# Sums of activations for the down-products: one set of hidden channels at a time, or two sets in one VectorE operation

## The chip, the cores and the metric

The kernel runs on one core of one Trainium2 chip. The metric is the device time in microseconds of one execution; lower is better. A run is called fast here when its time is within 1.5% of the fastest of the same kernel. TensorE is called PE in the profile, its weight loads PEld, VectorE DVE, ScalarE ACT, GpSimd POOL.

## The reference, cut to what matters

A linear-attention layer on 8 batches of 1024 tokens gives `x` (1024 x 512 for each batch). A mixer follows, and its second half is the part that matters here:

```python
h  = np.maximum(xt @ w_tok1, 0.0) @ w_tok2      # over tokens
u  = x + h.transpose(0, 2, 1)
h2 = np.maximum(u @ w_ch1, 0.0) @ w_ch2         # 512 -> 1536 -> 512 channels
return (u + h2).astype(np.float32)
```

## The kernel before

The two channel products are each made with seven products of half-size blocks in place of eight (a Strassen-Winograd scheme). The tokens are cut into 16 blocks `j`. In each, the 1536 hidden channels are done in three sets `m`: `up_set(j, m)` makes seven up-products into three PSUM banks (`x`, `y`, `z`), rectifies them into `G`, and makes the four sums of activations that the down-products need. Then `down_block(j)` makes seven down-products over all three sets. The title of the change speaks of heads; what it touches are these sets.

```python
SINGLE = 2
TOTALS = ((), (0, 1), (2,))
...
    def up_set(j, m):
        ...
        def total(n, a, b, add):
            f = nc.vector.tensor_add if add else nc.vector.tensor_sub
            c = slice(2 * both[0], 2 * both[-1] + 2)
            dve(
                512 * len(both), lambda: f(out=G[:, n, c], in0=G[:, a, c], in1=G[:, b, c]), ps=False,
                reads=[("G", j % 2, i, mm) for i in (a, b) for mm in both],
                writes=[("G", j % 2, n, mm) for mm in both],
            )
        ...   # seven up-products, rectified by ACT (relu) or DVE (add_relu) into G
        both = TOTALS[m] if SINGLE <= j < NSB - 1 else (m,)     # NSB = 16
        if both:
            total(3, 5, 2, True)
            total(5, 0, 5, False)
            total(4, 3, 0, False)
            total(6, 1, 4, False)
    ...
    def down_block(j):
        ...
                jobs.append(pe(
                    C2, 256, lambda t=t: mm(n, t),          # C2 = 6 matmuls
                    reads=w + [("G", j % 2, G_OF[n], m) for m in range(SETS)],   # all three sets
                    ...
        # order of the products: 1, 7, 6, 2, 5, 3, 4
```

Nothing is issued in the order in which it is written. `pe(...)`, `dve(...)` and `act(...)` add jobs with an assumed duration and dependences to a list, and a planner orders all of them on all engines before the program is built. So a change in one kind of job can change the order everywhere.

The softmax here doesn't subtract the row's maximum and nothing guards it: scores larger than these inputs give would overflow.

## Time and profile before

| | before |
|---|---|
| time, median of 3 runs | 423.13 us (423.12 to 423.6) |
| span in the profile | 421.2 us |
| TensorE busy | 412.1 us, 98% |
| VectorE busy | 348.0 us, 83% |
| sums of activations on VectorE | 52 of 1024 elements, 88 of 512 |

The lines are shown in the prediction. How to read them: in a group's line come line, engine, operation, output and inputs, shapes and count, then busy time in all, mean nanoseconds of one, and the idle time just ahead of them. In the trace of this kernel the printed duration of a VectorE operation reaches past the start of the next by 0.083 us (median of the 587 that are followed without a gap); for the wide sums the printed mean is 0.681 us and the median distance to the next start 0.602 us. What an operation takes from the engine is therefore read from the distance of two starts. An eviction is an operation of VectorE or ScalarE that reads a finished product out of its PSUM bank; the program lets the next product into that bank only after it.

### The profile page before, as it was taken

The page shows a single profiled execution, that of the slowest core. Times are in us where ns is not written, and L with a number is a line of the kernel's source. Part 1 is how long each engine was busy: PE and PEld are TensorE (multiplying, and loading weights), DVE is VectorE, ACT ScalarE, POOL GpSimd, SP SyncE. Part 2 cuts the span into 40 slices and gives each one's busy share as a digit, 9 for nine tenths or more (in the row PEclk, how much of TensorE's full clock was granted, in tenths as well). Part 3 has the DMA queues.
Part 4 walks back from the last instruction along what each step waited for, and adds up shares of the span by engine and source line. Part 5 has one row for each costly group of instructions (what it writes and reads, how often), then busy time and mean ns, then how long its engine had stood idle before and what let it go on. Part 6 is the DMA issues. An engine that isn't in the chain of part 4 may idle for free.

```text
span 421.2 us, 9421 instructions
## 1 busy us (share of the span) xinstructions
PE 412.1 (98%) x3838; PEld 347.7 (83%) x3838; DVE 348.0 (83%) x747; ACT 231.8 (55%) x444; POOL 66.2 (16%) x104
## 2 busy tenths in 40 slices
PE   7999999999999999999999999999999999999996
PEld 3587877688788888888798888888898899988885
DVE  2359969679679798988889899898988798997685
ACT  1858884475636546564645556655646645354530
POOL 8453220022003030022103020212100000010110
PEclk9999999999999999999999999999999999999999
DMA  9999999996975989398974989999760501250223
GB/s 166 207 201 206 207 206 164 225 177 140 216 145 103 195 133 235 64 186 141 207 163 94 191 139 224 163 200 179 153 146 0 152 27 76 50 151 2 102 100 103
DMA packets 96668, 62.48 MB, mean 148 GB/s; under 512 B 62064, under 2 KB 92272, under 8 KB 96624
## 3 DMA queue, kind: packets, MB, share of 16 engines
q0 software_dynamic: 34944, 45.09, 54.5%
q1 hardware_dynamic: 61056, 16.00, 21.6%
q10 hardware_dynamic: 624, 0.79, 0.7%
q8 instruction: 30, 0.49, 0.5%
q14 instruction: 14, 0.11, 0.1%
HBM read 59.24 MB, written 16.78 MB: 180 GB/s over the span
## 4 chain that ended last, share of the span: by engine, by line
PE 91%; DVE 4%; ACT 2%; DMA 1%; issue 0%; DVEq 0%
PE psum L1253 34%; PE psum L1144 33%; PE psum L848 4%; PE psum L484 4%; PE psum L597 3%; PE psum L964 3%; PE psum L656 2%; DMA o<-in_F_dram 1%; PE psum L620 1%; DVE u L1071 1%; PE psum L736 1%; PE psum L687 1%; PE psum L581 1%; PE psum L405 1%; PE psum L711 1%; PE psum L1032 1%
## 5 line engine op out<-in xcount | busy, mean ns | idle before, releaser
L1253 PEld LDWEIGHTS <-G 128*128 128x128 bf16 x1344 | 130.6, 98 | 19.7 <-issue 1.5
L1253 PE MATMUL psum<-wc_sb,G 128*128 128x256 bf16 x768 | 102.5, 273 | 0.5 <-ACT psum L1309 0.2
L1166 ACT ACTIVATE G<-psum 128x512 bf16<-128x512 f32 x96 | 57.3, 600 | 56.0 <-PE psum L1144 55.4
L1144 PEld LDWEIGHTS <-wc_sb 128*128 128x128 bf16 x768 | 73.8, 98 | 10.9 <-issue 0.6
L1253 PE MATMUL psum<-wT,G 128*128 128x256 bf16 x576 | 77.7, 273 | 0.1
L1180 DVE TENSOR_TENSOR G<-G 128x512 bf16<-128x512 bf16 (+1 forms) x140 | 69.5, 516 | 1.0
L1144 PEld LDWEIGHTS <-wT 128*128 128x128 bf16 x576 | 55.7, 98 | 9.0 <-issue 1.2
L1144 PE MATMUL psum<-uT,wc_sb 128*128 128x256 bf16 x384 | 57.7, 273 | 0.2 <-ACT psum L1187 0.2
L1144 PE MATMUL psum<-S,wc_sb 128*128 128x256 bf16 x384 | 57.6, 273 | 0.1
L1144 PE MATMUL psum<-S,wT 128*128 128x256 bf16 x384 | 55.6, 273 | 0.4 <-DVE S L781 0.4
L1287 POOL DMA_DIRECT2D out_dram<-o x30 | 16.4, 548 | 240.2 <-DVE o L1293 125.6
L1125 DVE CUSTOM_DVE_ANT_0 G<-psum,ub 128x512 bf16<-128x512 f32 x48 | 32.9, 685 | 15.3 <-PE psum L1144 15.1
L1172 ACT COPY ua<-psum 128x512 f32<-128x512 f32 x48 | 28.2, 588 | 30.1 <-PE psum L1144 29.7
L606 ACT ACTIVATE a<-psum 128x512 bf16<-128x512 f32 x64 | 36.4, 602 | 12.4 <-PE psum L597 11.8
L1293 DVE TENSOR_TENSOR o<-psum,u 128x512 f32<-128x512 f32 x55 | 37.5, 683 | 6.4 <-PE psum L1253 6.3
L1187 ACT COPY psum<-psum 128x512 f32<-128x512 f32 x48 | 27.8, 580 | 18.9 <-DVE G L1125 9.9
L1125 DVE CUSTOM_DVE_ANT_0 G<-psum,ua 128x512 bf16<-128x512 f32 x48 | 32.7, 682 | 5.0 <-ACT ua L1172 4.6
L1172 ACT COPY ub<-psum 128x512 f32<-128x512 f32 x48 | 28.2, 588 | 7.0 <-PE psum L1144 6.3
L1144 PE MATMUL psum<-uT,wT 128*128 128x256 bf16 x192 | 28.8, 273 | 0.1
L673 DVE TENSOR_TENSOR x_sb<-psum,rdn 128x512 bf16<-128x512 f32 x40 | 27.4, 686 | 0.6
L597 PE MATMUL psum<-qT,kT 128*128 128x512 bf16 x64 | 21.5, 380 | 0.6 <-ACT kT L549 0.6
L346 POOL DMA_DIRECT2D v_sb<-in_v_dram x18 | 13.5, 749 | 50.7 <-DMA uT<-u 48.0
(108 smaller groups left out, 547.2 us busy)
## 6 DMA issues: line engine op xcount, KB each, us to landing
out_dram<-o POOLq DMA_DIRECT2D x30, 512.0 KB, 4.2
k_sb<-in_k_dram POOLq DMA_DIRECT2D x14, 512.0 KB, 8.5
v_sb<-in_v_dram POOLq DMA_DIRECT2D x14, 512.0 KB, 10.3
q_sb<-in_q_dram POOLq DMA_DIRECT2D x14, 512.0 KB, 9.9
wc_sb<-in_moe_w_ch_dram POOLq DMA_DIRECT2D x6, 256.0 KB, 12.3
wc_sb<-in_moe_w_ch_dram POOLq DMA_DIRECT2D x4, 384.0 KB, 12.3
k_sb<-in_k_dram POOLq DMA_DIRECT2D x4, 256.0 KB, 6.8
v_sb<-in_v_dram POOLq DMA_DIRECT2D x4, 256.0 KB, 7.3
```

What stands on the lines that cost most here:

```text
L484: nc.tensor.matmul(t[0:KP, 0:hn], ET_sb[:, si, :], k_sb[:, hs, si, :], start=a, stop=z)
L597: lambda: nc.tensor.matmul(bank(bk), kT[:, h].rearrange("p c k -> p (c k)"), qT[:, h].rearrange("p j s -> p (j s)"), start=True, stop=True,),
L606: lambda: nc.scalar.activation(out=a_t[h // 2 % 2][:, h % 2], in_=bank(bk), func=ACT.Exp, scale=scale),
L673: lambda: nc.vector.tensor_tensor(out=x_sb[:, :, h * D : (h + 1) * D].rearrange("p (n c) d -> p n c d", n=2), in0=view()[:, :, :, 0:D], in ...
L1125: nc.vector._custom_dve(TENSOR_ADD_SAT, out=out, in0=in0, in1=in1, s0=FMAX, s1=0.0)
L1144: nc.tensor.matmul(t[:, c, :], w1_of(n, dd, 2 * m + c), a_of(j, n, dd), start=(n in (1, 7) and c == 0 and dd == 0), stop=(c == 1 and dd == 1),
L1166: lambda: nc.scalar.activation(out=G[:, n, cs], in_=view(src), func=ACT.Relu),
L1172: 512, lambda: nc.scalar.copy(out=dst, in_=view("y")), writes=[(name, s % 2)],
L1180: 512 * len(both), lambda: f(out=G[:, n, c], in0=G[:, a, c], in1=G[:, b, c]), ps=False,
L1187: 512, lambda: nc.scalar.copy(out=view("y"), in_=view("x")), takes=[bk["y"]],
L1253: nc.tensor.matmul(to, G[:, G_OF[n], cc, t * P : (t + 1) * P], w2_of(n, cc), start=(n in opens and (t == 0 or alone) and cc == 0), stop=(c ...
L1293: 512, lambda: nc.vector.tensor_add(out=dst, in0=view(src), in1=u_of(sh, dh)),
```

## The change

Its intent: never make the sums for two sets in one operation, so that those of set 0 can run earlier and each piece is shorter. The whole diff is one number, which makes the condition on `j` false for every block:

```diff
-SINGLE = 2
+SINGLE = 99
 TOTALS = ((), (0, 1), (2,))
```

## The prediction

The trace of the kernel before shows the pace: behind a matmul of 256 columns the median distance to the next start is 0.109 us (0.109 to 0.110 from the 10th to the 90th percentile).

> **What bounds the kernel now.** I read the page's first part first, then the busy time by stage, then the groups of TensorE by shape, then stretches of the timeline, and last the list of waits.
>
> ```profile
> PE 412.1 (98%) x3838; PEld 347.7 (83%) x3838; DVE 348.0 (83%) x747; ACT 231.8 (55%) x444; POOL 66.2 (16%) x104
> ...
> PE 91%; DVE 4%; ACT 2%; DMA 1%; issue 0%; DVEq 0%
> ```
>
> TensorE (PE) is busy for 98% of the span and carries 91% of the chain that ended last. VectorE (DVE), the engine that the change loads, is second with 83%. The stages, with the columns of busy microseconds by engine:
>
> ```profile
> core 0: us, PE busy (x) PEld busy (x) DVE busy (x) ACT busy (x) POOL busy (x), PEclk, DMA share, GB/s
> 0.00:60.00 60.00, 55.83 (x598) 41.92 (x599) 39.25 (x109) 41.35 (x92) 26.67 (x43) 1.00 1.20 198
> 60.00:400.00 340.00, 339.19 (x3090) 290.95 (x3088) 293.99 (x610) 186.45 (x346) 38.43 (x59) 1.00 0.73 143
> 400.00:421.20 21.20, 17.08 (x155) 14.82 (x153) 14.77 (x29) 4.00 (x7) 1.07 (x2) 1.00 0.28 100
> ```
>
> From 60 to 400 us TensorE is idle for 340 - 339.19 = 0.8 us in all, with a granted clock of 1.00. VectorE is busy there for 293.99 / 340 = 86%. A busy TensorE need not be at its peak, so I checked the pace in the timeline of TensorE:
>
> ```profile
> 183.17 0.60 PE L1144 MATMUL psum<-S,wT 128*128 128x256 bf16 x4
> 183.61 0.60 PE L1144 MATMUL psum<-uT,wc_sb 128*128 128x256 bf16 x4
> 184.04 0.60 PE L1144 MATMUL psum<-S,wc_sb 128*128 128x256 bf16 x4
> 184.48 0.82 PE L1253 MATMUL psum<-wc_sb,G 128*128 128x256 bf16 x6
> ...
> 186.00 0.82 PE L1253 MATMUL psum<-wT,G 128*128 128x256 bf16 x6
> ```
>
> Four matmuls of 256 columns start 0.44 us apart (183.17 to 183.61), so 0.109 us each, and the next group starts with no gap. The up-products (L1144) and the down-products (L1253) have 1344 of them each; 2688 x 0.109 = 293 us, 70% of the span. The middle of this kernel is a dense stream of matmuls, and only what opens a gap in it, or lengthens the start or the tail, can move the time.
>
> [...] The timeline of VectorE:
>
> ```profile
> 175.59 0.68 DVE L1180 TENSOR_TENSOR G<-G 128x1024 bf16<-128x1024 bf16 x1
> 176.19 0.68 DVE L994 TENSOR_TENSOR u<-psum,x_sb 128x512 bf16<-128x512 f32 x1
> ...
> 184.45 0.42 DVE L1180 TENSOR_TENSOR G<-G 128x512 bf16<-128x512 bf16 x1
> 184.78 0.42 DVE L781 TENSOR_TENSOR S<-uT,S 128x512 bf16<-128x512 bf16 x1
> ```
>
> A wide sum takes 176.19 - 175.59 = 0.60 us of the engine, a narrow one 184.78 - 184.45 = 0.33 us. Taken over all places in the trace where such a sum has a direct successor, the medians are 602 and 336 ns. The printed 0.68 and 0.42 have some 0.08 us of tail under the next operation. [...]
>
> **The change part by part.** There are 16 blocks, each with three sets of hidden channels (the "heads" of the change's title are these sets: a third of the columns of the up-weights), and each block needs four sums of activations for the seven-product scheme. Blocks 0, 1 and 15 make them set by set already: 3 x 3 x 4 = 36 narrow operations. Blocks 2 to 14 make them for sets 0 and 1 together after set 1 and for set 2 alone: 13 x 4 = 52 wide and 52 narrow. The groups by shape have exactly this:
>
> ```profile
> L1180 DVE TENSOR_TENSOR G<-G 128x512 bf16<-128x512 bf16 x88 | 35.3, 418 | 0.7
> L1180 DVE TENSOR_TENSOR G<-G 128x1024 bf16<-128x1024 bf16 x52 | 35.2, 681 | 0.3
> ```
>
> Removed: 52 wide sums, 52 x 0.602 = 31.3 us of VectorE. Added: 104 narrow ones, 104 x 0.336 = 34.9 us. Net +3.6 us over the run, 0.28 us per block of about 23.4 us (the wide sums of blocks 2 and 14 lie 281 us apart, over 12 blocks), or 1.2% of VectorE. By printed durations the group would grow by 104 x 0.418 - 52 x 0.681 = 8.1 us, but 0.08 us of each of the 52 extra ones lies under a neighbour. VectorE then goes from 294 to about 297.6 us busy in the 340 us, 87.5%. Idle time of the engine is 46 us there, so the 3.6 us fit without becoming the bound.
>
> Moved: the sums of set 0 may now run once its own rectified products exist, about 8 us (a third of a block) before those of set 1. That makes no product ready sooner, because each down-product sums over all three sets and so waits for set 2. In the block shown, the wide sums stood at 175.59 to 179.26, and the first product that reads one (L1253 with wT) starts at 186.00, so they had 6 us or more to spare; set 2's sum at 184.45 had about one. The tight one is not changed in shape. A narrow sum also holds the in-order VectorE for 0.34 us where a wide one held it for 0.60, so an eviction that becomes ready behind it is later by 0.27 us less.
>
> Moved too: the kernel orders all its work by a planner before it is built, so other durations and dependences give another order on every engine from block 2 on. The TensorE work is the same, 3838 matmuls. On the path that sets the end, the sum is 0 us from the work itself, plus what the new order opens or closes in gaps.
>
> **The rivals.** First, *VectorE becomes the bound in its fullest stretches*. For it: it is at 18.8 to 19.0 of 20 us in three of the 20-us stretches (160 to 180 and 220 to 260), where 0.24 us more per 20 us is a sixth to a fifth of what is left. Its lateness would appear as PSUM banks freed late, so TensorE gaps. If the whole 3.6 us came through, the time would be 426.7. Against: the list of waits has TensorE waiting for hardly any VectorE work after the start:
>
> ```profile
> PE psum L1144 <- DVE S L781: 0.4, 1, 0.4
> PE psum L1253 <- ACT psum L1309: 0.2, 1, 0.2
> PE psum L1144 <- ACT psum L1187: 0.2, 1, 0.2
> PE psum L1253 <- DVE o L1293: 0.2, 1, 0.2
> ```
>
> and one wait of 0.4 us of a weight load for a sum (L1180). So a delay of some tenths is mostly taken up by the other PSUM banks; I expect 0 to 1 us of it.
>
> Second, *finer pieces help*: sums of set 0 fill small idle times earlier, and evictions wait less. What speaks against a large gain is the ceiling: 0.8 us of idle TensorE in the middle, so at best about 422.3.
>
> Third, *the new order meets an accident*: a transposed load or an eviction in another turn, and a single TensorE gap of one to several microseconds, or a longer tail than now. The page cannot exclude it. The old setting was presumably chosen because it was no slower, which leans me the same way. That would make 424 to 427. The tail itself belongs to block 15, which is set by set in both kernels.
>
> **Range and chances.** The work on TensorE gives 423.1 unchanged. I add 0.3 us for VectorE's load and 0.3 us for the mean harm of a new order, which is my guess between "nothing" and the third rival. So I predict 423.7 us, 8 times in 10 between 422.3 (all middle gaps closed) and 426.2 (most of the added 3.6 us on the path). A gain of 2% would be 8.5 us, ten times the idle there is to win in the middle: chance 0.01. A loss of 2% needs more than twice the added VectorE time on the path: 0.03. Within 2%: 0.96.
>
> **What would show it.** In the changed kernel the sums should be one group of 192 narrow operations of about 418 ns with no wide ones; VectorE's busy time near 351.6 us (+3.6) in 799 instructions; TensorE with the same 3838 matmuls and 412 to 413 us busy; and the idle of TensorE from 60 to 400 us still under 2 us. If that idle grew to 3 us or more with waits for VectorE evictions (L1125, L1293, L994) or for ACT copies behind them, the first rival is right. If one wait of over a microsecond stood for the difference, or one for a DMA, it is the third. If the first 60 or the last 20 us changed in length by more than 0.5 us, my view that only the middle is touched is wrong.

Three statements in it rest on readings that it does not print; all are from the trace of the kernel before. That a busy TensorE need not be at its peak: from 60 to 400 us the starts of matmuls come late by 3.9 us in all against the trace's own pace, where the stage shows 0.8 us of idle time. That VectorE works in order: all 747 operations start in the order of the built program (in the changed kernel all 799). That other PSUM banks take up a delay: from 60 to 400 us there are 322 cases in which VectorE was the last to read a bank, and the next matmul into that bank started 0.59 us (median) after VectorE's printed end, in 275 cases at least 0.3 us after it. That this takes up most of a delay was an estimate; the experiments give the price.

## The result

The changed kernel took 422.80 us (median of 4 runs, 422.75 to 423.41), the kernel before 423.22 us (4 runs). The ratio of the fast runs is 0.9992, with a 95% interval of 0.9975 to 1.0009: no difference shown. A ratio here is formed within the rounds in which both kernels ran, so it is not quite the ratio of the medians quoted. A second comparison, in the experiments, gave 1.0005.

The page and the stages (0 to 60, 60 to 400 and the end) of the changed kernel:

```profile
PE 411.3 (98%) x3820; PEld 347.7 (83%) x3838; DVE 352.3 (84%) x799; ACT 231.2 (55%) x444; POOL 66.2 (16%) x104
```

```profile
0.00:60.00 60.00, 55.67 (x592) 41.66 (x597) 39.19 (x109) 41.17 (x91) 26.67 (x43) 1.00 1.20 199
60.00:400.00 340.00, 338.32 (x3076) 291.00 (x3088) 298.89 (x664) 186.01 (x347) 38.49 (x59) 1.00 0.73 142
```

The sums, by shape, in its groups:

```profile
L1180 DVE TENSOR_TENSOR G<-G 128x512 bf16<-128x512 bf16 x192 | 77.1, 421 | 2.6
```

Where they stand, in its timeline of VectorE; this is the block whose wide sums stood at 175.59 to 179.26 before:

```profile
166.27 0.41 DVE L1180 TENSOR_TENSOR G<-G 128x512 bf16<-128x512 bf16 x1
166.60 0.68 DVE L1000 TENSOR_TENSOR u<-psum,a 128x512 bf16<-128x512 f32 x1
167.20 0.42 DVE L1180 TENSOR_TENSOR G<-G 128x512 bf16<-128x512 bf16 x1
```

VectorE has 799 - 747 = 52 operations more and is busy 352.3 - 348.0 = 4.3 us more. The first sums of this block run 9.3 us earlier (166.27 against 175.59). TensorE, which carries the chain to the end, is as full as it was: 338.32 of 340 us in the middle against 339.19. The 0.9 us between them are partly a gap in the record: the trace after has 3820 matmul records and 3838 weight loads, so 18 matmuls that ran are missing. The change did to VectorE all that it was meant to do, and the time did not move.

### The profile page after: what moved, and what is told of

The parts are those of the page before. It is cut to its first block, busy times and chain, and to the rows that moved or that the text cites. A ratio compares the mean times of both kernels' runs of the same rounds, so it can differ in the third digit from the quotient of the medians.

```text
span 421.4 us, 9457 instructions
## 1 busy us (share of the span) xinstructions
PE 411.3 (98%) x3820; PEld 347.7 (83%) x3838; DVE 352.3 (84%) x799; ACT 231.2 (55%) x444; POOL 66.2 (16%) x104
## 4 chain that ended last, share of the span: by engine, by line
PE 89%; DMA 4%; DVE 3%; issue 1%; POOL 1%; ACT 1%; POOLq 0%; DVEq 0%
PE psum L1253 35%; PE psum L1144 34%; PE psum L848 5%; PE psum L964 4%; PE psum L484 3%; DMA q_sb<-in_q_dram 3%; PE psum L597 2%; PE psum L656 2%; DMA v_sb<-in_v_dram 2%; DVE u L1071 1%; PE psum L687 1%; PE psum L620 1%; PE psum L736 1%; PE psum L711 1%; PE psum L581 1%
## 5 line engine op out<-in xcount | busy, mean ns | idle before, releaser
L1253 PEld LDWEIGHTS <-G 128*128 128x128 bf16 x1344 | 130.2, 98 | 19.5 <-issue 1.6
L1253 PE MATMUL psum<-wc_sb,G 128*128 128x256 bf16 x768 | 103.0, 273 | 0.6 <-DVE wait L1293 0.4
L1144 PEld LDWEIGHTS <-wc_sb 128*128 128x128 bf16 x768 | 74.2, 98 | 10.3 <-issue 0.3
L1180 DVE TENSOR_TENSOR G<-G 128x512 bf16<-128x512 bf16 x192 | 77.1, 421 | 2.6
L1253 PE MATMUL psum<-wT,G 128*128 128x256 bf16 x576 | 77.5, 273 | 0.5
L1144 PEld LDWEIGHTS <-wT 128*128 128x128 bf16 x576 | 55.7, 98 | 10.0 <-issue 1.4
L1144 PE MATMUL psum<-uT,wc_sb 128*128 128x256 bf16 x384 | 57.7, 273 | 0.1
L1144 PE MATMUL psum<-S,wc_sb 128*128 128x256 bf16 x384 | 57.6, 273 | 0.2
L1144 PE MATMUL psum<-S,wT 128*128 128x256 bf16 x384 | 56.1, 273 | 0.5 <-DVE S L781 0.4
L1125 DVE CUSTOM_DVE_ANT_0 G<-psum,ub 128x512 bf16<-128x512 f32 x48 | 33.0, 687 | 15.7 <-PE psum L1144 15.4
L1125 DVE CUSTOM_DVE_ANT_0 G<-psum,ua 128x512 bf16<-128x512 f32 x48 | 33.1, 689 | 11.0 <-ACT ua L1172 10.7
L1293 DVE TENSOR_TENSOR o<-psum,u 128x512 f32<-128x512 f32 x55 | 37.6, 686 | 1.9 <-PE psum L1253 1.5
L1144 PE MATMUL psum<-uT,wT 128*128 128x256 bf16 x192 | 28.8, 273 | 0.2
L346 POOL DMA_DIRECT2D k_sb<-in_k_dram x18 | 13.6, 758 | 62.0 <-PE psum L964 33.0
```

The source lines that it names most:

```text
L346: return lambda: nc.gpsimd.dma_start(out=dst, in_=src)
L1125: nc.vector._custom_dve(TENSOR_ADD_SAT, out=out, in0=in0, in1=in1, s0=FMAX, s1=0.0)
L1144: nc.tensor.matmul(t[:, c, :], w1_of(n, dd, 2 * m + c), a_of(j, n, dd), start=(n in (1, 7) and c == 0 and dd == 0), stop=(c == 1 and dd == 1),
L1253: nc.tensor.matmul(to, G[:, G_OF[n], cc, t * P : (t + 1) * P], w2_of(n, cc), start=(n in opens and (t == 0 or alone) and cc == 0), stop=(c ...
L1293: 512, lambda: nc.vector.tensor_add(out=dst, in0=view(src), in1=u_of(sh, dh)),
```

## The experiments

Two theories stood at first. *Theory 1*: TensorE's stream sets the time, VectorE has room, so 3.6 us of VectorE work more is nearly free. *Rival*: VectorE's time is on the path, and a new planned order won it back by luck. Twelve further runs were made, in three groups; each group shares one chip and its runs of the kernel before. In all kernels except the third, fourth, eleventh and twelfth, a comparison of the built programs shows the order of work on every engine kept as in the kernel that they start from: only the named operations differ.

### The added work alone, without a new order (e1) and the change again (e2)

The first kernel starts from the kernel before. The planner still sees one wide sum, but two narrow operations are issued in its place. What this document calls the fixed cost of an operation is the difference between the two, from the medians of starts in the trace of before: 2 x 0.336 - 0.602 = 0.07 us.

```diff
+        def parts(f, n, a, b):
+            for mm in both:
+                c = slice(2 * mm, 2 * mm + 2)
+                f(out=G[:, n, c], in0=G[:, a, c], in1=G[:, b, c])
...
-                512 * len(both), lambda: f(out=G[:, n, c], in0=G[:, a, c], in1=G[:, b, c]), ps=False,
+                512 * len(both), lambda: parts(f, n, a, b), ps=False,
```

> The kernel before with its planned order left as it is on every engine; only where a wide sum stood, two narrow ones are issued back to back. This adds the 52 fixed costs (3.6 us of VectorE) without any new order. Theory (TensorE's dense stream is the bound, VectorE has room): 423.0 to 423.7 us, ratio within 0.2% of the kernel before. Rival (the added VectorE time is on the path, and in the changed kernel the new order won it back): about 426.8 us, ratio 1.0085.

Measured: 423.79 us (6 runs) against 423.17 (11 runs), ratio 1.0015, interval 1.0002 to 1.0028. The added work alone costs 0.0015 x 423.2 = 0.6 us (0.1 to 1.2). Its profile's page has VectorE at 350.9 us, 2.9 us over before. The rival's 426.8 is excluded.

> The changed kernel once more, for a narrower interval beside the first experiment. Theory: 422.6 to 423.4, ratio 0.998 to 1.001. Rival (there is a real gain of finer pieces): a ratio clear of 1, at about 0.999.

Measured: 423.48 us (6 runs), ratio 1.0005, interval 0.9992 to 1.0018. There is no gain, and the interval overlaps that of the first kernel. So it is not shown that the new order won anything back; if it did, it was some tenths of a microsecond.

### Half of the change (e3), and the other direction (e4)

```diff
-SINGLE = 2
+SINGLE = 8
```

> Set-by-set sums in blocks 0 to 7 and 15, pairs in blocks 8 to 14: another planned order with half of the change. It shows how much a new order alone scatters. Theory: within 0.7 us of 423.2. Rival (a new order can by accident open gaps of microseconds): 424.5 or more, with a TensorE wait of over 1 us in the middle.

Measured: 424.97 us (4 runs), ratio 1.0042, interval 1.0024 to 1.0060. This was a miss: half of the change is slower by 1.8 us than none of it, where all of it is not. The stage from 300 to 400 us of the profile shows where at least a part lies. First the kernel before, then this one:

```profile
300.00:400.00 100.00, 100.00 (x923) 88.96 (x920) 84.38 (x167) 51.25 (x95) 4.80 (x9) 1.00 0.31 84
```

```profile
300.00:400.00 100.00, 99.12 (x909) 87.70 (x908) 85.61 (x169) 51.78 (x95) 4.81 (x9) 1.00 0.33 84
```

TensorE had no idle time there before and has 0.88 us here, and 908 weight loads in place of 920 have begun. No single wait of TensorE reaches a microsecond: the longest in this stage are of 0.4 us. So what I expected of the rival, one long wait, was not what happened; it was several short gaps.

The place says what the loss is not. The trace of this kernel has only narrow sums up to 232.5 us (blocks 0 to 7), and wide sums from 245.7 to 390.0 us. Up to 300 us it has begun 603 + 2167 = 2770 weight loads, the kernel before 2767, so the half with the split sums had lost nothing by then. The loss (1.1 us of span in this profiled run, the fastest of the four) fell in blocks that make their sums in pairs as before, and only the order of work is another there. What in that order opens the gaps is not shown.

The fourth kernel makes the sums of blocks 2 to 14 for all three sets in one operation, after the last set:

```diff
-TOTALS = ((), (0, 1), (2,))
+TOTALS = ((), (), (0, 1, 2))
```

> The other direction: in blocks 2 to 14 the four sums are made for all three sets in one operation after set 2 (52 operations of 1536 elements, estimated at 0.87 us each, in place of 52 wide and 52 narrow ones; about 3.6 us of VectorE less). Theory (VectorE's amount of work does not count, but when the sums of the last set end does): no gain; the second down-product needs two sums, 1.7 us in place of 0.7, so slower by 0 to 1 us in each block where the planner finds nothing to put between: 423 to 430 us, most likely 424.5. Rival (VectorE's amount of work counts): 420 to 422 us.

Measured: 424.62 us (4 runs), ratio 1.0032, interval 1.0019 to 1.0045. (The 0.87 us expected of a sum of three sets goes on from the medians of before: 0.602 + (0.602 - 0.336).) VectorE has less to do (343.5 us busy, 4.5 less than before), and the kernel is slower by 1.4 us. The list of waits of TensorE in this kernel has a line that is larger than before (0.2 us, once):

```profile
PE psum L1253 <- ACT psum L1309: 1.1, 3, 0.7
```

L1253 are the down-products, and L1309 is the copy that opens their second bank after the first product. The down-products wait more for the start of a block's chain here. That late sums delay it is not shown, and the record speaks against it: the copy follows the first product, which reads none of the four sums, and the copy's own wait for a sum is 1.8 us, once, in both kernels. This kernel is also a new order, and the new order of the third run lost 1.8 us. So the cause of the 1.4 us stays open, and the run is no test of what less VectorE work is worth.

### How much is a microsecond of VectorE worth? (e5, e6)

The changed kernel, with VectorE additions on spare data that nobody reads behind some of the sums, and the planner not told. An addition has the shape of a narrow sum, and in the trace it takes the same 0.33 us from start to start.

```diff
+MORE = {3: 0, 5: 0, 4: 0, 6: 1}     # fifth run; the sixth has 4: 1 too
...
+    spare_t = tile_of([P, 2, S2], BF16, "spare")
+    nc.vector.memset(spare_t, 0.0)
...
+        def with_more(f, n, a, b, c):
+            f(out=G[:, n, c], in0=G[:, a, c], in1=G[:, b, c])
+            for _ in range(MORE[n]):
+                nc.vector.tensor_add(out=spare_t[:, 0], in0=spare_t[:, 1], in1=spare_t[:, 1])
```

> The changed kernel in its own order, with an independent VectorE addition of 512 bf16 elements on spare data behind one of the four sums of each set: 48 operations, 16 us of VectorE more, four and a half times what the change added. Theory (room on VectorE): VectorE in the middle rises from 299 to about 314 of 340 us; the time rises by less than 2 us, to 423 to 425. Rival (added VectorE time is on the path): 439.

Measured: 427.99 us (4 runs), ratio 1.0105, interval 1.0071 to 1.0139; a miss, dearer than theory 1 said (under 2 us).

> The same behind two of the four sums: 96 operations, 32 us of VectorE more. VectorE would have to be busy 329 of 340 us in the middle. Theory: the room begins to run out, since work comes in bursts; 425 to 434 us, with TensorE gaps behind evictions. Rival (all on the path): 455.

Measured: 434.67 us (4 runs), ratio 1.0265, interval 1.0231 to 1.0300: just past the upper end of what theory 1 gave. Both rivals' figures (439 and 455) are far off. The stages from 60 to 400 us of the two (fifth first):

```profile
60.00:400.00 340.00, 337.64 (x3055) 287.42 (x3053) 308.49 (x699) 184.45 (x343) 38.51 (x59) 1.00 0.74 143
```

```profile
60.00:400.00 340.00, 334.48 (x3010) 282.14 (x3010) 315.60 (x732) 181.75 (x340) 37.43 (x57) 1.00 0.72 139
```

VectorE is not full even in the second (315.6 of 340), and yet TensorE's idle time rose from 0.8 us to 2.4 and 5.5. What it waits for stands in the waits list of the sixth run:

```profile
PE psum L1147 <- DVE G L1128: 2.7, 7, 0.9
...
PE psum L623 <- DVE x_sb L640: 0.7, 2, 0.4
...
PE psum L1261 <- DVE o L1301: 0.6, 2, 0.4
```

(The added lines shift the numbers: L1147 is L1144 of before, L1128 is L1125, L623 is L620, L640 is L637, L1261 is L1253, L1301 is L1293.) Up-products wait for the rectifying operation that empties their PSUM bank, and the attention and down-products for theirs. Before, the list had no line of the first kind at all. So VectorE time reaches TensorE through PSUM banks that come free late, in many small pieces.

The chain of work that ended last says the same. Its shares by engine in the fifth and the sixth run:

```profile
PE 70%; DVE 24%; ACT 2%; issue 2%; DMA 1%; DVEq 0%
```

```profile
PE 58%; DVE 34%; DMA 4%; issue 2%; ACT 1%; POOL 1%; DVEq 0%; POOLq 0%
```

VectorE had 4% of it in the kernel before and 3% in the changed one.

These gaps account for the loss. I summed, from the trace, by how much each matmul's successor started later than the trace's own pace, the median distance of starts behind a matmul of so many columns (in the kernel before 0.109 us for 256, 0.216 for 512 and 0.057 for 130), counting distances of more than 5 ns and leaving out the first 60 us. The kernel before has 4.1 us of such gaps, the fifth run 8.0 and the sixth 14.1; the spans grew by 4.0 and 11.2 us. If each gap is put down to the instruction whose semaphore came last before it, VectorE ended 1.4 us of them before, 5.4 in the fifth run (27 gaps) and 11.5 in the sixth (41 gaps). That is the whole growth, and most of these gaps are too short for the waits list.

### Does it matter where the work stands? (e9, e10)

*Theory A*: ahead of the last set's sums VectorE's work is free, because those sums have 6 us or more to spare. *Theory B*: it costs the same anywhere. The same 48 additions as in the fifth run:

```diff
+MORE = {3: 0, 5: 1, 4: 1, 6: 1}
...
+            for _ in range(MORE[n] if m == 1 else 0):     # ninth run; the tenth has m == 2
```

> The changed kernel in its own order with the same 48 spare additions (16 us of VectorE) as the fifth run, but all behind the sums of set 1, three in each block, where the wide sums stood and the trace of before shows 6 us to spare. Theory A (what counts is where the work stands: before the last set's sums there is room): 423 to 424.5. Theory B (each microsecond of VectorE costs some 0.3 us wherever it stands): 428, as the fifth run.

Measured: 427.25 us (6 runs) against 423.29 (11 runs), ratio 1.0088, interval 1.0068 to 1.0108.

> The same 48 additions, all behind the sums of set 2, just ahead of the block's down-products and the next block's S sums, three in each block. Theory A: dearer than the fifth run, 429 to 434. Theory B: 428.

Measured: 428.06 us (6 runs), ratio 1.0103, interval 1.0081 to 1.0125. The two intervals overlap, and both contain the fifth run's 1.0105. Theory A fell: the spare time of the sums themselves is not spare time of VectorE, since evictions behind them in the queue are delayed too. In the ninth run's trace the gaps that VectorE ended are 5.2 us in place of 1.4; 2.8 us of them stand behind two evictions, L1128 (rectifying) and L676 (attention).

### Told to the planner (e11), and a new order alone (e12)

The eleventh run is the fifth with the additions' time given to the planner; the twelfth is the kernel before with one assumed delay changed, and no work added:

```diff
-                512 * len(both), lambda: with_more(f, n, a, b, c), ps=False,
+                512 * len(both) + 647 * MORE[n], lambda: with_more(f, n, a, b, c), ps=False,
```

```diff
-    LAG = {"PE": 0.25, "DVE": 0.15, "ACT": 0.15, "POOL": 0.2, "DMA": 1.0}
+    LAG = {"PE": 0.25, "DVE": 0.16, "ACT": 0.15, "POOL": 0.2, "DMA": 1.0}
```

> The fifth run's kernel (one spare addition behind one sum of each set), but with the planner told of their time, so that it orders all engines around them. Theory (the planner finds places for added VectorE work, which is why the change, planned anew, cost nothing): 423 to 425.5. Rival (no order can hide it, VectorE's bursts are the limit): 427.5 or more.

Measured: 427.20 us (4 runs), ratio 1.0086, interval 1.0060 to 1.0111. The planner's new order hides nearly nothing that the old order did not (1.0105, overlapping). The median lies between the two expectations, nearer to the rival's.

> The kernel before with one number of the planner moved (the assumed delay behind a VectorE operation 0.16 in place of 0.15 us): the same instructions in another order, no work added or taken. It measures what a new order alone does. Theory (orders scatter by some tenths of a per cent, the old one was picked as a good one): 423 to 425.5. Rival (order does not matter, so the third run's +1.8 us came from its half of the change): within 0.4 us of the kernel before.

Measured: 423.38 us (6 runs), ratio 0.9994, interval 0.9974 to 1.0013, though about a third of the rows of TensorE's program moved. So this new order cost nothing. By itself that speaks for the rival, that the third run's loss came from its half of the change. But the price of VectorE time below puts that half (24 of 52 splits, 1.7 us) at 0.3 to 0.6 us, not 1.8, and in the third run's trace the loss stands where the sums are as before. So an unlucky order is the likelier cause there, though no run repeats the third run's order without its split sums. One harmless order is not a measure of the scatter.

### Is TensorE the bound? (e7, e8)

Both kernels with one of six matmuls left out of each down-product of blocks 2 to 13, order kept. Their outputs are wrong, which doesn't matter for the times.

```diff
-            for cc in range(C2):
+            less = 1 if 2 <= j <= 13 else 0
+            for cc in range(C2 - less):
```

> A wrong result on purpose: the kernel before, its order kept, with one of the six matmuls left out of every down-product of blocks 2 to 13 (168 matmuls of 0.109 us, 18.3 us of TensorE). Theory (TensorE's stream is the bound): the time falls by nearly all of it, to 405 to 407 us, with VectorE 91% busy in the middle. Rival (VectorE or the transfers set the pace as well): 412 us or more.

Measured: 412.21 us (4 runs) against 423.12 (7 runs), ratio 0.9740, interval 0.9704 to 0.9777. Of the 18.3 us taken from TensorE, 0.026 x 423.1 = 11.0 us came off the time. It is what the rival said and not theory 1. The stage from 60 to 400 us of this run:

```profile
60.00:400.00 340.00, 337.56 (x3022) 283.91 (x3020) 301.97 (x628) 189.70 (x353) 39.51 (x61) 1.00 0.75 146
```

The idle time of TensorE is 2.4 us in place of 0.8, and the gaps from start to start are 11.4 us in place of 4.1. These 7.3 us are what is missing of the 18.3. Counted as for the sixth run, VectorE ended 7.8 us of the gaps in place of 1.4 and transfers 0.05, so of the rival's two causes it is mostly VectorE. In the chain that ended last its share is 25%, against 4% before:

```profile
PE 64%; DVE 25%; DMA 4%; ACT 2%; issue 2%; POOL 1%; POOLq 0%; DVEq 0%
```

The order was still the one planned for the full matmuls; a new one was not tried.

> A wrong result on purpose: the changed kernel with the same matmuls left out, so that VectorE (about 92.5% in the middle) is closer to the bound. Theory: 405 to 408 us; if fixed costs begin to count here, it is 0.5 to 2 us slower than the seventh run, else within 0.5 us of it. Rival (finer pieces help where VectorE is fuller): 0.5 to 2 us faster than the seventh run.

Measured: 413.01 us (4 runs), ratio 0.9749, interval 0.9721 to 0.9778. The median is 0.8 us above the seventh run's, but the intervals lie almost on each other, so this one is inconclusive.

### What the runs say together

| run | added to VectorE | from the ratio | per us added |
|---|---|---|---|
| e1, fixed costs of the change | 3.6 us | +0.6 us | 0.17 |
| e9, after set 1 | 16.1 us | +3.7 us | 0.23 |
| e11, planned | 16.1 us | +3.6 us | 0.23 |
| e10, after set 2 | 16.1 us | +4.4 us | 0.27 |
| e5, one behind each set | 16.1 us | +4.4 us | 0.28 |
| e6, two behind each set | 32.3 us | +11.2 us | 0.35 |

The added times are counts by 0.336 us (52 by 0.07 for e1). All rows but e1 start from the changed kernel, but the ratios are to the kernel before; the two are taken as equal here (0.9992 and 1.0005). The rows' intervals are wide: 0.02 to 0.33 per us for e1, 0.18 to 0.28 for e9, 0.30 to 0.39 for e6. Only e6 is shown to differ from others, from e9 and e11. A microsecond of VectorE costs about 0.2 to 0.35 us of the kernel, and a microsecond of TensorE brought 11.0 / 18.3 = 0.6 us. Neither engine alone is the bound: TensorE sets most of the time, and VectorE part of it through the PSUM banks.

## Why the prediction was right

**Counts and durations.** Predicted: 192 narrow sums of about 418 ns, 799 VectorE operations, 351.6 us busy. The profile shows 192 of 421 ns, 799 and 352.3 us. TensorE has 411.3 us in place of 412 to 413, with 18 records missing and the same 3838 weight loads; its idle time from 60 to 400 us is 1.7 us, under the 2 us allowed. One reading is slightly off: 0.24 us of the 1.0 to 1.2 us left in the fullest stretches is a fifth to a quarter, not a sixth to a fifth.

**Off the path.** Predicted: 0 to 1 us through VectorE, 0.3 us taken. The first run isolates this term and gives 0.6 us (0.1 to 1.2). The term was of the right size, but the reason given for it was too easy. The prediction set 46 us of idle VectorE time against 3.6 us of work and concluded that it fits. The fifth to eleventh runs show that work put onto VectorE does not fall into that idle time for free. The change was harmless because it is small: 3.6 us at 0.2 to 0.35 each is 0.7 to 1.3 us, 0.3 per cent at most.

**Spare time of the sums.** The step "they had 6 us or more to spare" is true of the sums and not of the engine; the ninth run put work in that very place and paid 3.7 us for 16.1.

**First rival** (VectorE as the bound, 426.7 us): it would have taken a price of 1, and the runs show 0.17 to 0.35. Its mechanism, PSUM banks freed late, is the one that the fifth and sixth runs show; only its size was wrong for this change. **Second rival** (finer pieces help): two comparisons, 0.9992 and 1.0005, show no gain. The eighth run, made to bring VectorE nearer to its limit, shows none either. **Third rival** (a new order meets an accident): it did not happen to the changed kernel. Nothing in the prediction excluded it, so this is luck as far as the record tells. It probably happened to the half-way kernel, 1.8 us slower, as several short gaps and not as one long one; at 424.97 us that would still have lain in the range. The 0.3 us allowed for it was a guess, and nothing here measures it.

**The bound.** "Only what opens a gap in it can move the time" held: the added gaps account for the losses in the fifth and sixth runs. What was missing is that gaps also open when the stream gets shorter, as the seventh run shows. The ceiling of 0.8 us for a gain was also read too low: busy times hide gaps, since a matmul's printed 0.27 us reaches past the next start at 0.109 us, and by the distance of starts there were 4.1 us after the first 60.

**The range.** 422.80 us lies in 422.3 to 426.2, and near its lower end; the middle was 0.9 us too high. "Nothing changes" lies in that range too, so the number alone tests the mechanism little. The 0.6 us that I added for load and a new order is smaller than the scatter of single runs of the kernel before (422.6 to 425.5 us over all groups).

## What to carry to other kernels

In this kernel a fixed cost for each operation (0.07 us) had to be multiplied by its count (52) and then by a price below 1 (0.17 to 0.35); the price can be measured by adding operations on spare data, which takes one kernel. A nearly idle-free first engine and a short list of waits did not mean that the second engine was free, because its lateness returned as many gaps of 0.2 to 0.3 us, which show in the distance of starts. And grouping over sets is worth little on its own: it saves 0.07 us a pair here. When it went on until all the sums come after the last set, the kernel was 1.4 us slower although VectorE had less to do; whether the late sums or the new order did that is open.
